# Three of twelve output projections by seven products of quarters instead of eight (Strassen, one level)

## The chip, the cores and the metric

The kernel runs on one core of a Trainium2 chip. The metric is device time in microseconds for one execution; 8 runs of the kernel before are given by their median. A core has a matrix engine (TensorE, PE in the profile), a vector engine (DVE), a scalar engine (ACT), GpSimd (POOL) and a queue engine that issues DMAs (SP). Each engine works through its own queue in order; semaphores hold an instruction until its inputs are there. Matmuls write to PSUM[...]; everything else here is in SBUF.

## What is computed

Four batches, eight heads, 768 tokens, head dimension 64. Queries and keys are each assigned to one of 16 clusters; attention is masked to pairs of the same cluster. The result, 3072 tokens by 512, goes through a two-layer network. All of it is f32.

```python
scores = np.where(mask, scale * np.matmul(q, k.transpose(0, 1, 3, 2)), -1e9)
attn = softmax(scores); x = (attn @ v) as (B*S, H*D)     # 3072 x 512
h = x @ w_in                                             # 512 -> 2048
sp = np.maximum(h, 0.0) + np.log1p(np.exp(-np.abs(h)))
g = h * erf(sp)
out = g @ w_out                                          # 2048 -> 512
```

The change is in the last line, `g @ w_out`.

## The kernel before

Heads are worked in 16 pairs (p), each in two halves of 384 queries and six key tiles of 128: a "unit" is one pair, half and key tile, 192 in all. Attention's outputs land transposed in tiles `xT`. The two-layer network works on chunks of 256 tokens, three to a batch, twelve in all (`NCHUNK = 12`, `CPB = 3`, `TB = 256`); chunks 9, 10 and 11 are the last batch's.

For a chunk n, `hidden(n)` (line 599) makes the hidden layer: eight groups of two 128-row feature tiles, each the sum of four matmuls 256 columns wide into a PSUM tile `hp`, which DVE copies into the tile `g` (16 feature tiles x 256 tokens; two buffers). After the last group `gate(n)` (line 567) puts Softplus and Erf on ACT, half a chunk at a time, and multiplies on POOL; chunk 11's products are on DVE. `project(n)` (line 623) then makes the output: for each of two token tiles, 16 matmuls 512 columns wide add up in one PSUM bank `po`, DVE copies it to `osb`, and SP stores it. `w_out` is a resident tile of 16 feature tiles by 512.

The order of the network's matmuls comes from one generator, `ffn_stream` (line 643). It runs hidden(n) and, after the first 16 matmuls, slips in two matmuls of project(n-1) behind each one of hidden(n). While attention runs, this stream is drawn in portions (`pump`) between units; after the last unit, a closing loop draws the rest: by the plan's count that is chunk 8's projection and the hidden layers and projections of chunks 9, 10 and 11. The first part of the program is pinned to the written order (`InOrder`, `in_order`); from there on a planner orders each engine's queue, with the written order as priority, and puts in all waits.

The tiles that the change borrows belong to attention: `prs` (eight tiles of exponentials, two planes of 384 each), `lows` (bf16 operands of query and key), `rowp` (transposed queries and keys, two buffers of each), `vp` (values, two buffers), `accp` (row sums, two buffers), `stage` (loaded queries and keys), and in PSUM `ps_s` (scores, two buffers of two banks). Operations made through `InOrder` all carry line 61 in the profile, so groups there are told apart by their tiles.

Of the kernel before, what the change touches and what calls it, by code (L numbers as in the profile page):

```python
# [9 lines left out]
F32 = mybir.dt.float32  # L10
# [4 lines left out]
ALU = mybir.AluOpType  # L15
# [4 lines left out]
P = 128  # L20
B, H, S, D = 4, 8, 768, 64
C = 16
NJ = S // P
Q = 32
NB = S // Q
HW = S // 2
HJ = NJ // 2
HP = H // 2
NPAIR = B * HP
DM, DFF = H * D, 2048  # L30
NFT = DFF // P
GW = 2
TB = 256
NCHUNK = B * S // TB
# [35 lines left out]
def kernel(  # L70
# [10 lines left out]
    nc = tc.nc  # L81

    in_order = [True]
    te, ve, ae, ge = (
        InOrder(tc, e, in_order) for e in (nc.tensor, nc.vector, nc.scalar, nc.gpsimd)
    )

    def pool(name, bufs, **kw):
        return ctx.enter_context(tc.tile_pool(name=name, bufs=bufs, **kw))

    const = pool("const", 1)
    stage = pool("stage", 1)
    vp = pool("vp", 2)
    rowp = pool("rowp", 2)
    routep = pool("routep", 1)
    small = pool("small", 2)
    accp = pool("accp", 2)
# [4 lines left out]
    ps_s = pool("ps_s", 2, space=PSUM)  # L102
# [10 lines left out]
    w_out = const.tile([P, NFT, DM], F32, name="w_out")  # L113
# [6 lines left out]
    lows = [  # L120
        {nm: const.tile([P, 2, S], BF16, name=f"{nm}m{i}") for nm in "qk"} for i in range(2)
    ]

    prs = [const.tile([P, 2, HW + 2], F32, name=f"pr{i}") for i in range(NPT)]
# [46 lines left out]
    for base, pattern, sign, op, fill in (  # L171
# [5 lines left out]
            out=first, in_=first, compare_op=op, fill=fill, base=base, pattern=pattern,  # L177
# [94 lines left out]
    for it in range(2):  # L272
# [4 lines left out]
            out=twice, in0=ss, scalar=inv, in1=norm, op0=ALU.mult, op1=ALU.add  # L277
# [3 lines left out]
            out=norm, in0=twice, scalar1=0.5, scalar2=(1e-6 if it else 0.0),  # L281
# [240 lines left out]
    def divide(u):  # L522

        p, half, _ = units[u]
        st = pairs[p]
        av = st["av", half]

        psum = ps_x.tile([P, HW], F32, name="psum", tag="x")
        for e in range(2):
            te.matmul(  # L530
                psum[e * D : (e + 1) * D], lhsT=minus, rhs=st["acc", half][:, e], start=True, stop=True
            )

        inv = routep.tile([P, HW], F32, name="inv")
        den = routep.tile([P, HW], F32, name="den")
        ae.activation(out=inv, in_=psum, func=ACT.Ln, bias=alleps, scale=-1.0)
        ae.activation(out=inv, in_=inv, func=ACT.Exp, scale=-1.0)
        yield
        ve.scalar_tensor_tensor(
            out=den, in0=psum, scalar=S * EPS, in1=inv, op0=ALU.subtract, op1=ALU.mult  # L540
        )
        ve.scalar_tensor_tensor(
            out=den, in0=den, scalar=2.0, in1=inv, op0=ALU.add, op1=ALU.mult
        )
        x = xTs.setdefault(p, {})
        lo = half * HW
        while lo < (half + 1) * HW:
            c = lo // TB
            hi = min((c + 1) * TB, (half + 1) * HW)
            if c not in x:  # L550
                x[c] = xTp.tile([P, TB], F32, name=f"xT{c}", bufs=XBUFS[c])
            mine = slice(lo - half * HW, hi - half * HW)
            ve.scalar_tensor_tensor(
                out=x[c][:, lo - c * TB : hi - c * TB], in0=av[:, mine], scalar=av[:, HW : HW + 1],
                in1=den[:, mine], op0=ALU.add, op1=ALU.mult,
            )
            lo = hi
        done.add((p, half))
        if half == 1:
            del pairs[p]  # L560
        yield


    TJ = TB // P
    CPB = S // TB
# [25 lines left out]
    def gate_products(n=NFT):  # L591
        for product in gating[:n]:
            product()
        del gating[:n]

    gs = {}
    resting = [0]

    def hidden(n):
        b, c = n // CPB, n % CPB  # L600
        gs[n] = gp.tile([P, NFT, TB], F32, name="g")
        for fp in range(NFT // GW):
            while converted[0] < DM // P * (fp * GW * P // LC + 1):
                yield None
            hp = ps_x.tile([P, GW, TB], F32, name="hp", tag="x")
            for a in range(GW):
                f0 = (fp * GW + a) * P
                for r in range(HP):
                    te.matmul(
                        hp[:, a], lhsT=w_in[:, r, f0 : f0 + P],  # L610
                        rhs=xTs[b * HP + r][c],
                        start=(r == 0), stop=(r == HP - 1),
                    )
                    if (a, r) != (GW - 1, HP - 1):
                        yield 4 * TB
            ve.tensor_copy(out=gs[n][:, fp * GW : (fp + 1) * GW], in_=hp)
            if fp == NFT // GW - 1:
                gate(n)
            yield 4 * TB

    out_v = out.rearrange("(b j p) m -> b j p m", p=P, j=NJ)

    def project(n):
        b, c = n // CPB, n % CPB
        gate_products()
        for tt in range(TJ):
            po = ps_x.tile([P, DM], F32, name="po", tag="x")
            for ft in range(NFT):
                while converted[0] < n_w_in + ft + 1:
                    yield None  # L630
                te.matmul(
                    po, lhsT=gs[n][:, ft, tt * P : (tt + 1) * P], rhs=w_out[:, ft],
                    start=(ft == 0), stop=(ft == NFT - 1),
                )
                if ft < NFT - 1:
                    yield 4 * DM
            osb = outp.tile([P, DM], F32, name="osb")
            ve.tensor_copy(out=osb, in_=po)
            nc.sync.dma_start(out=out_v[b, c * TJ + tt], in_=osb)
            yield 4 * DM  # L640
        del gs[n]

    def ffn_stream():


        late = iter(())
        for n in range(NCHUNK):
            b, c = n // CPB, n % CPB
            halves = range(c * TB // HW, ((c + 1) * TB - 1) // HW + 1)
            while not all((b * HP + r, h) in done for r in range(HP) for h in halves):  # L650
                yield None
            i = 0
            for cost in hidden(n):
                yield cost
                i += cost is not None
                if n > 1 and i > 2 * GW * HP:
                    for _ in range(2):
                        if (x := next(late, None)) is not None:
                            yield x
            yield from late  # L660
            late = project(n)
        yield from late

    stream = ffn_stream()
    pumped = [0]

# [35 lines left out]
    for e in range(2):  # L702
        ve.tensor_copy(
            out=ccT[e * D : (e + 1) * D, :, e * C : (e + 1) * C],
            in_=pct[e * D : (e + 1) * D].rearrange("d (r e c) -> d r e c", e=2, c=C)[:, :, e],
# [11 lines left out]
    for e in range(2):  # L717
        ve.reduce_sum(
            out=own[:, e : e + 1],
            in_=ident.rearrange("p (g x c) -> p x g c", x=2, c=C)[:, e], axis=AX.XY,  # L720
# [13 lines left out]
    for slot in range(2 * NJ * HP):  # L734
        in_order[0] = slot < FIRST
        p, r = divmod(slot, 2 * NJ)
# [40 lines left out]
    for u in range(2 * NJ * HP, len(units), 2):  # L777
        p, half, j = units[u]
# [24 lines left out]
        attend(n)  # L803
    for _ in divide(len(units) - 1):
        pass
    while next(stream, None) is not None:
        pass

# [31 lines left out]
```

## Time and profile before

| | |
|---|---|
| median of 8 runs | 1198.52 us (1193.54 to 1200.39) |
| profiled execution | 1199.88 us, of which the span is 1198.2 us |
| granted TensorE clock, mean over the span | 0.984 |
| matmuls of the hidden layer (`hp`) | 1536 records, 388.5 us busy |
| matmuls of the projections (`po`) | 768 records, 367.8 us busy |
| last attention matmul, in the trace | about 1001.5 us |
| projections of chunks 9, 10, 11 | 1064.0 to 1098.0, 1119.1 to 1153.1, 1166.9 to 1194.5 us; the first two interleaved with the next hidden layer |
| last store issued | 1195.28 us |

The span runs from the first to the last instruction; the rest of the execution's time lies around it. One f32 matmul of the code leaves two records. "Busy" is the union of the records of a group, "mean" the length of one record, and matmuls overlap in the pipeline: the spacing of starts, not the mean length, is what one costs in a row. In the forty slices a digit is the busy share in tenths.

### The profile page before, as it was taken

What the parts mean: (1) busy time and instruction counts of PE and PEld (TensorE: products, weight loads), DVE (VectorE), ACT (ScalarE), POOL (GpSimd) and SP (SyncE); (2) the same over time, 40 slices, a digit from 0 to 9 for tenths busy, and PEclk for the clock granted to TensorE, in tenths of its full rate; (3) what the DMA queues carried; (4) which work ended last, traced back from release to release, by engine and by line L of the source; (5) the groups of instructions that cost most, each with busy time, mean ns of one, the idle gap of its engine ahead of it and who ended that gap; (6) DMA issues with size and microseconds to landing.
All of it is one profiled execution on the core that took longest, in us unless ns stands there. A gap on an engine that the chain in (4) does not pass through costs nothing.

```text
span 1198.2 us, 13349 instructions
## 1 busy us (share of the span) xinstructions
PE 1151.5 (96%) x4912; PEld 619.8 (52%) x4912; DVE 515.8 (43%) x971; ACT 587.3 (49%) x682; POOL 461.6 (39%) x466
## 2 busy tenths in 40 slices
PE   4999978999999989999999999999999999999998
PEld 1233356654544554564474455565456456576663
DVE  7778885635443544343462434334354012111121
ACT  5889897863525363471553454164355253222222
POOL 3677764554333424161353243144244253031100
PEclk8999989899999899999999999999999999999999
DMA  7652443110202010020201101020000000000000
GB/s 137 164 128 40 99 152 58 53 27 23 43 15 27 23 27 22 9 40 1 45 14 17 35 14 33 9 36 14 10 23 1 9 9 1 18 1 18 8 10 18
DMA packets 140561, 42.95 MB, mean 36 GB/s; under 512 B 133328, under 2 KB 133328, under 8 KB 140496
## 3 DMA queue, kind: packets, MB, share of 16 engines
q1 hardware_dynamic: 137360, 41.70, 15.6%
q10 hardware_dynamic: 3136, 0.39, 0.3%
q8 instruction: 39, 0.64, 0.2%
q14 instruction: 26, 0.21, 0.1%
HBM read 35.68 MB, written 6.29 MB: 35 GB/s over the span
## 4 chain that ended last, share of the span: by engine, by line
PE 78%; ACT 8%; issue 7%; DVE 4%; DMA 2%; SPq 0%; POOL 0%; ACTq 0%; DVEq 0%; POOLq 0%
PE hp L61 25%; PE po L61 25%; PE sc L61 13%; PE av L61 8%; PE sm L61 4%; ACT w_out L61 2%; ACT L61 2%; DVE nmx L61 1%; ACT km L61 1%; PE psim L61 1%; PE psum L61 1%; DMA in_q<-in_q_dram 1%; ACT pr L61 1%; ACT inv L61 1%; ACT a_s L61 1%
## 5 line engine op out<-in xcount | busy, mean ns | idle before, releaser
L61 PE MATMUL hp<-xT,w_in 128*128 128x256 f32 x1536 | 388.5, 390 | 7.9 <-DVE xT L61 6.2
L61 PE MATMUL po<-w_out,g 128*128 128x512 f32 x768 | 367.8, 597 | 0.6 <-DVE den L61 0.6
L61 PEld LDWEIGHTS hp<-xT,w_in 128*128 128x128 f32 x1536 | 290.1, 194 | 130.0 <-issue 84.4
L61 POOL TENSOR_TENSOR acc<-acc,pr 128x384 f32<-128x384 f32 x256 | 236.3, 954 | 290.5 <-ACT pr L61 290.3
L61 DVE TENSOR_REDUCE nmx<-sm 128x1 f32<-128x384 f32 x384 | 195.8, 550 | 148.0 <-PE sm L61 147.1
L61 ACT ACT_TABLE_LOAD x110 | 141.1, 1283 | 231.9 <-DVE g L61 128.8
L61 ACT ACTIVATE pr<-sc 128x768 f32<-128x768 f32 x192 | 147.0, 806 | 147.1 <-PE sc L61 146.9
L61 PEld LDWEIGHTS po<-w_out,g 128*128 128x128 f32 x768 | 141.8, 190 | 106.9 <-issue 94.1
L61 POOL TENSOR_TENSOR g<-a_s,g 128x512 f32<-128x512 f32 x88 | 111.4, 1298 | 216.5 <-ACT a_s L61 216.5
L61 PE MATMUL sc<-qT,kT 64*128 64x384 f32 x768 | 181.8, 528 | 4.8 <-ACT pr L61 4.7
L61 DVE COPY g<-hp 128x512 f32<-128x512 f32 x96 | 65.9, 687 | 255.1 <-PE hp L61 254.7
L61 PE MATMUL av<-pr,in_v 128*64 128x386 f32 x768 | 139.9, 496 | 0.0
L61 PE MATMUL sm<-km,qm 128*128 128x384 bf16 x384 | 103.2, 336 | 14.4 <-DVE nmx L61 4.1
L61 PEld LDWEIGHTS sc<-qT,kT 64*128 64x128 f32 x768 | 69.9, 188 | 82.3 <-issue 47.0
L61 POOL TENSOR_TENSOR acc<-pr,pr 128x384 f32<-128x384 f32 x64 | 65.4, 1043 | 92.8 <-ACT pr L61 92.8
L61 PEld LDWEIGHTS av<-pr,in_v 128*64 128x64 f32 x768 | 49.2, 136 | 80.1 <-issue 70.1
L61 PEld LDWEIGHTS <-qm 128*128 128x128 bf16 x384 | 34.8, 99 | 81.8 <-issue 66.8
L61 DVE SCALAR_TENSOR_TENSOR den<-psum,inv 128x384 f32<-128x384 f32 x32 | 17.8, 557 | 129.2 <-ACT inv L61 128.8
L61 ACT ACTIVATE w_out<-w_out 128x512 int32<-128x512 uint32 (+2 forms) x68 | 62.0, 952 | 2.1 <-DMA w_out<-in_moe_w_out_dram 1.7
L61 ACT ACTIVATE a_s<-g 128x2048 f32<-128x2048 f32 x24 | 45.8, 1910 | 32.5 <-DVE g L61 32.3
L61 PE MATMUL sc<-qm,km 64*128 64x384 bf16 x384 | 60.1, 328 | 0.0
L61 ACT COPY nmT<-pn 6x128 bf16<-6x128 bf16 x31 | 7.7, 248 | 95.1 <-PE pn L61 95.1
(75 smaller groups left out, 605.5 us busy)
## 6 DMA issues: line engine op xcount, KB each, us to landing
w_out<-in_moe_w_in_dram SPq DMA_DIRECT2D x16, 512.0 KB, 6.6
in_q<-in_q_dram SPq DMA_DIRECT2D x64, 96.0 KB, 3.1
in_v<-in_v_dram SPq DMA_DIRECT2D x32, 192.0 KB, 3.0
w_out<-in_moe_w_out_dram SPq DMA_DIRECT2D x12, 512.0 KB, 3.6
out_dram<-osb SPq DMA_DIRECT2D x24, 256.0 KB, 2.0
in_k<-in_k_dram SPq DMA_DIRECT2D x60, 96.0 KB, 3.4
qm<-nmT SPq DMA_DIRECT2D x186, 0.2 KB, 1.7
a_s<-in_moe_w_out_dram SPq DMA_DIRECT2D x4, 512.0 KB, 3.4
```

The costliest lines, as they stand in the source:

```text
L61: ins = getattr(self.engine, name)(*args, **kw)
```

## The change

For chunks 9, 10 and 11 `project` is replaced by `project_fast`. It cuts `g` in quarters (token tile x feature half) and `w_out` in quarters (feature half x output half), and makes the four output quarters from seven products of sums and differences of quarters. Each product is eight matmuls 256 wide.

- `add_weights`, written after the last unit and ahead of the closing loop, makes three sums of weight quarters (24 adds of 128x256, every fourth on POOL) in planes of `prs` and `lows`.
- `subtract_weights`, written after chunk 8's projection, replaces two weight quarters in place by differences.
- `add_hidden(n)`, at the head of each `project_fast(n)`, makes three sums of hidden quarters (in tiles of `rowp`, or of `vp` and `accp`) and replaces two quarters of `g` in place by differences, all on DVE.
- The products are collected in the two `ps_s` buffers and put together by DVE in two tiles of `stage`; an output quarter is stored as soon as it is done, so a chunk has four stores of 128x256 instead of two of 128x512.
- The hidden layers of chunks 10 and 11 have no projection slipped in; each projection runs in one piece behind the next hidden layer.

```diff
+    FAST = NCHUNK - CPB
+    HF, HM = NFT // 2, DM // 2
+    def g_part(n, tt, fh):
+        return gs[n][:, fh * HF : (fh + 1) * HF, tt * P : (tt + 1) * P]
+    def w_part(fh, mh):
+        return w_out[:, fh * HF : (fh + 1) * HF, mh * HM : (mh + 1) * HM]
...
+    def add_weights():
+        planes = [t[:, e, 0:HM] for t in prs for e in range(2)]
+        planes += [
+            t[nm].bitcast(F32)[:, e, 0:HM] for t in lows for nm in "qk" for e in range(2)
+        ]
+        for name, (x, y) in {"++": ((0, 0), (1, 1)), "0+": ((0, 0), (0, 1)), "1+": ((1, 0), (1, 1))}.items():
+            w_sum[name] = [planes.pop(0) for _ in range(HF)]
+            for f in range(HF):
+                (ge if f % 4 == 3 else ve).tensor_tensor(
+                    out=w_sum[name][f], in0=w_part(*x)[:, f], in1=w_part(*y)[:, f], op=ALU.add
+                )
+    def subtract_weights():
+        for x, y in (((0, 1), (1, 1)), ((1, 0), (0, 0))):
+            for f in range(0, HF, 2):
+                ve.tensor_tensor(
+                    out=w_part(*x)[:, f : f + 2], in0=w_part(*x)[:, f : f + 2],
+                    in1=w_part(*y)[:, f : f + 2], op=ALU.subtract,
+                )
+    def add_hidden(n):
+        if n % 2:
+            tiles = [rowp.tile([P, S], F32, name=nm + "T") for nm in "qkqk"]
...
+        lot = S // P
+        sums = g_sum[n] = {}
+        for i, (name, x, y) in enumerate(
+            (("+1", (1, 0), (1, 1)), ("0+", (0, 0), (0, 1)), ("++", (0, 0), (1, 1)))
+        ):
...
+            for fs, o in ((slice(0, lot), tiles[i]), (slice(lot, HF), tiles[3][:, rest])):
+                ve.tensor_tensor(out=o, in0=g_part(n, *x)[:, fs], in1=g_part(n, *y)[:, fs], op=ALU.add)
+        for x, y in (((1, 0), (0, 0)), ((0, 1), (1, 1))):
+            ve.tensor_tensor(out=g_part(n, *x), in0=g_part(n, *x), in1=g_part(n, *y), op=ALU.subtract)
+    def project_fast(n):
...
+        add_hidden(n)
...
+        def product(o, g, w):
+            for f in range(HF):
+                te.matmul(
+                    o, lhsT=g[f] if isinstance(g, list) else g[:, f],
+                    rhs=w[f] if isinstance(w, list) else w[:, f], start=(f == 0), stop=(f == HF - 1),
+                )
+                yield 4 * HM
...
+        yield from product(m3, g_part(n, 0, 0), w_part(0, 1))
+        yield from product(m4, g_part(n, 1, 1), w_part(1, 0))
+        yield from product(m2, gsum["+1"], w_part(0, 0))
+        yield from product(m5, gsum["0+"], w_part(1, 1))
+        ve.tensor_copy(out=so_far(0, 1), in_=m3)
+        ve.tensor_copy(out=so_far(0, 0), in_=m4)
+        put(1, 0, so_far(0, 0), m2, ALU.add)
+        put(1, 1, so_far(0, 1), m2, ALU.subtract)
+        put(0, 1, so_far(0, 1), m5, ALU.add)
+        put(0, 0, so_far(0, 0), m5, ALU.subtract)
...
+        yield from product(m6, g_part(n, 1, 0), w_sum["0+"])
+        yield from product(m7, g_part(n, 0, 1), w_sum["1+"])
+        put(1, 1, so_far(1, 1), m6, ALU.add)
+        put(0, 0, so_far(0, 0), m7, ALU.add)
+        yield from product(m1, gsum["++"], w_sum["++"])
+        for tt in range(TJ):
+            put(tt, tt, so_far(tt, tt), m1, ALU.add)
+            nc.sync.dma_start(
+                out=out_v[b, c * TJ + tt, :, tt * HM : (tt + 1) * HM], in_=so_far(tt, tt)
+            )
+        del gs[n]
...
-                if n > 1 and i > 2 * GW * HP:
+                if 1 < n <= FAST and i > 2 * GW * HP:
...
-            late = project(n)
+            if n == FAST:
+                subtract_weights()
+            late = (project if n < FAST else project_fast)(n)
...
+    add_weights()
     while next(stream, None) is not None:
```

More of the change, by code (lines that the diff above doesn't have):

```diff
@@ L641, in project @@
         del gs[n]
+    FAST = NCHUNK - CPB
[4 more added lines that the diff above has]
+        return w_out[:, fh * HF : (fh + 1) * HF, mh * HM : (mh + 1) * HM]
+    w_sum = {}
+    g_sum = {}
+    def add_weights():
[9 more added lines that the diff above has]
+                )
@@ new lines, in subtract_weights @@
+    def subtract_weights():
[8 more added lines that the diff above has]
+            tiles = [rowp.tile([P, S], F32, name=nm + "T") for nm in "qkqk"]
+        else:
+            tiles = [vp.tile([P, NJ, 2, D], F32, name="in_v") for _ in range(2)]
+            tiles = [t.rearrange("p j e d -> p (j e d)") for t in tiles]
+            tiles += [
+                accp.tile([P, 2, HW], F32, name="acc").rearrange("p e n -> p (e n)") for _ in range(2)
+            ]
+        tiles = [t.rearrange("p (f t) -> p f t", t=P) for t in tiles]
+        lot = S // P
[3 more added lines that the diff above has]
+        ):
+            rest = slice(i * (HF - lot), (i + 1) * (HF - lot))
+            sums[name] = [tiles[i][:, f] for f in range(lot)] + [tiles[3][:, f] for f in range(rest.start, rest.stop)]
+            for fs, o in ((slice(0, lot), tiles[i]), (slice(lot, HF), tiles[3][:, rest])):
+                ve.tensor_tensor(out=o, in0=g_part(n, *x)[:, fs], in1=g_part(n, *y)[:, fs], op=ALU.add)
+        for x, y in (((1, 0), (0, 0)), ((0, 1), (1, 1))):
+            ve.tensor_tensor(out=g_part(n, *x), in0=g_part(n, *x), in1=g_part(n, *y), op=ALU.subtract)
@@ new lines, in project_fast, with put, so_far @@
+    def project_fast(n):
+        b, c = n // CPB, n % CPB
+        add_hidden(n)
+        gsum = g_sum[n]
+        one = ps_s.tile([P, 2, 512], F32, name="sc", tag="s").rearrange("p e (h m) -> p (e h) m", h=2)
+        two = ps_s.tile([P, 2, 512], F32, name="sc", tag="s").rearrange("p e (h m) -> p (e h) m", h=2)
+        osb = [
+            stage.tile([P, NB, Q], F32, name="in_" + nm).rearrange("p n t -> p (n t)")[:, 0:DM] for nm in "qk"
+        ]
+        def product(o, g, w):
[5 more added lines that the diff above has]
+                yield 4 * HM
+        def put(tt, mh, x, y, op):
+            ve.tensor_tensor(out=osb[tt][:, mh * HM : (mh + 1) * HM], in0=x, in1=y, op=op)
+        def so_far(tt, mh):
+            return osb[tt][:, mh * HM : (mh + 1) * HM]
+        m3, m4, m2, m5 = (one[:, i] for i in range(4))
+        m6, m7, m1 = (two[:, i] for i in (0, 1, 2))
+        yield from product(m3, g_part(n, 0, 0), w_part(0, 1))
[10 more added lines that the diff above has]
+            nc.sync.dma_start(
+                out=out_v[b, c * TJ + tt, :, (1 - tt) * HM : (2 - tt) * HM], in_=so_far(tt, 1 - tt)
+            )
[4 more added lines that the diff above has]
+        yield from product(m1, gsum["++"], w_sum["++"])
+        for tt in range(TJ):
+            put(tt, tt, so_far(tt, tt), m1, ALU.add)
+            nc.sync.dma_start(
+                out=out_v[b, c * TJ + tt, :, tt * HM : (tt + 1) * HM], in_=so_far(tt, tt)
+            )
+        del gs[n]
```

## The prediction

> **What bounds the kernel now.** I read the share of busy time first, then the forty slices, then the stretch that the change touches, then the chain of waits at the end.
>
> ```profile
> PE 1151.5 (96%) x4912; PEld 619.8 (52%) x4912; DVE 515.8 (43%) x971; ACT 587.3 (49%) x682; POOL 461.6 (39%) x466
> PE   4999978999999989999999999999999999999998
> DVE  7778885635443544343462434334354012111121
> PEclk8999989899999899999999999999999999999999
> ```
>
> TensorE is the bound on average, and the slices say more: from slice 33 of 40 on PE is full, its clock is full, and VectorE (DVE) is at a tenth or two. That last stretch is where the change lies. By stretches there (columns: length; busy time and instructions of PE, weight loads, DVE, ACT, POOL; granted clock; DMA share; GB/s):
>
> ```profile
> 1057.00:1084.00 27.00, 27.00 (x90) 16.83 (x89) 3.36 (x5) 6.39 (x4) 4.94 (x4) 1.00 0.03 10
> 1084.00:1111.00 27.00, 27.00 (x100) 18.69 (x99) 3.46 (x5) 6.39 (x4) 4.94 (x4) 1.00 0.03 10
> 1139.00:1167.00 28.00, 28.00 (x105) 19.58 (x104) 5.86 (x9) 6.39 (x4) 0.00 (x0) 1.00 0.03 10
> ```
>
> PE never stops, and every other engine is idle for four fifths of the time. The chain that ended last closes it (start, length, what):
>
> ```profile
> 1153.24 13.81 PE hp L61 x64
> 1167.05 27.48 PE po L61 x64
> 1194.53 0.02 issue
> 1194.56 0.69 DVE osb L61
> ```
>
> Nothing but matmuls, one behind the other, then one copy and the last store. So a matmul taken out of this stretch comes off the end time in full, as long as nothing new makes PE wait.
>
> **The sum on TensorE.** The trace has two records for each f32 matmul of the code. One projection is 2 token tiles x 16 matmuls 512 wide = 32 matmuls = the 64 records of 27.48 us: 0.8588 us each. A matmul 256 wide is known from the hidden layer: 64 records, 32 matmuls, 13.81 us: 0.4316 us each, with a new weight tile at every one, as the new products have. Check: from 1043.05 us (end of chunk 8's projection, in the chain) to 1194.53 there lie 160 hidden matmuls and 96 of projection: 160 x 0.4316 + 96 x 0.8588 = 151.5 us, and the stretch is 151.48. The two prices explain all of it.
>
> After the change a projection is 7 products x 8 matmuls = 56, 256 wide: 56 x 0.4316 = 24.17 us. Saved per projection 27.48 - 24.17 = 3.31 us; three of them: **9.93 us**. One eighth of the work is 12.5%; of 27.48 us I get 12.0%, because two 256-wide matmuls (0.8632) cost 4 ns more than one 512-wide.
>
> A rule of the Trainium skill speaks against cutting matmuls in half: "TensorE: Matmul & The Clock Gate", section "Back-to-back issue gap", has a fixed cost of about 2.5 ns in each pass beside N/2.4, and "FP8 and Floating Point Precision", section "TensorE Precision Notes", counts 4 passes for true f32. By the rule, as an estimate, 512 wide is 4 x 215.8 = 863 ns and 256 wide 4 x 109.2 = 437 ns: 32 x 0.863 - 56 x 0.437 = 3.15 us saved, 9.5 in all. The rows give 9.9. The floor is there in the trace, but smaller (4 ns, not 10), and I take the rows.
>
> Start of a product: 21 products begin behind waits on sums, where a hidden group of four matmuls begins behind a PSUM buffer. The 98 records at 1042.89 took 21.15 us in the chain, 0.4316 each across some twelve such starts, so a start costs nothing that can be seen. Upper bound: the 0.17 us by which a closed run of 64 records outlasts its share of the chain (13.98 against 13.81), x 21 = 3.6 us. I take 0, the nearer row.
>
> **The sums, and what hides them.** No add of two SBUF f32 tiles of these widths runs in the trace. The nearest row is the gate's product, 128x512, 686 ns alone and 0.63 us in a row (4 in 2.50); from it I estimate 0.63 x width/512 + 0.05: 256 wide 0.37, 768 wide 1.0, 1024 wide 1.3 us. (From the other side 0.48, the 128x256 operation that reads PSUM.)
> - add_weights: 18 adds on DVE, 18 x 0.37 = 6.6 us, and 6 on POOL at some 0.7 (954 ns for 384 wide), 4 us. They come after the last attention products, about 1001 us. From 1010 to 1024 us DVE and POOL do nothing before; the sums are wanted some 80 us later. POOL's last four gate products of chunk 8 (1003.2 to 1008.2) can slip by 2 to 3 us; the projection that reads them starts at 1008.95 with other quarters. Cost 0.
> - subtract_weights: 8 of 512 wide, 5 us on DVE, once chunk 8's projection has read w_out (1043). First needed at 1084. Cost 0.
> - add_hidden, each chunk: 3 x (1.0 + 0.37) + 2 x 1.3 = 6.7 us of DVE. Now the timetable. The hidden layers of chunks 10 and 11 are no longer interleaved with projections, so PE runs chunk 9's rest to 1056.9, hidden 10 to 1084.5, projection 9 to 1108.7, hidden 11 to 1136.3, projection 10 to 1160.5, projection 11 to 1184.6. A gate is done 12 us after its last hidden matmul where POOL multiplies (1057 to 1069.1), about 10 where DVE does (0.7 + 6.4 of ACT + 2.5). So the sums of 9 are ready at 1069 + 6.7 = 1076 (wanted at 1084.5), of 10 at 1103 (1136.3), of 11 at 1146 + 6.7 = 1153 (1160.5). Slack 8, 33 and 8 us. Cost 0; and products m3 and m4, which need no sum of the hidden layer, cover another 16 x 0.4316 = 6.9 us.
>
> A second rule is against this: "GPSIMD Engine Reference", section "Specifications", says that POOL shares its SBUF interfaces with DVE instructions that have two SBUF inputs, and all these adds have two. The gate of chunk 9 has eight POOL products, 9.9 us by the row; if DVE's 5 us of weight subtraction stopped POOL outright, chunk 9's sums would come at 1081 rather than 1076: still before 1084.5. Rule and row give the same end time.
>
> - Stores: six more of 256 columns, each some 0.36 us on SP's queue, which in this stretch holds nothing else. Cost 0.
> - Hidden buffers: there are two, so hidden 11 needs chunk 9's buffer, free after m7; m1 and the first hidden group (8 matmuls each, 6.9 us together) lie between that and its first write. Cost 0.
> - PSUM: the products use the two score buffers, free since attention ended; each is read by DVE at least 8 us before the next projection writes it.
> - The end: before, one copy of 0.69 us and one store (issued in 0.33 us). After, two DVE adds of a 256-wide PSUM half (0.48 each by the row of that width) and two stores of half the size; the second leaves 0.27 us later. Bounds -0.1 and +0.6; I take **+0.3 us**.
>
> Sum: 9.93 - 0.3 = 9.6 us off the span of 1198.2, so 1188.6; the profiled execution took 1199.88, which makes 1190.3. The median of the runs is 1.36 us below that execution: **1189.0 us**.
>
> **Rivals.** All turn on the order in DVE's queue. As the code is written, the sums of chunk n come behind all copies and gate products of hidden layer n+1. The order executed is not the written one:
>
> ```profile
> 1156.73 0.69 DVE L61 COPY g<-hp 128x512 f32<-128x512 f32 x1 [2.76 <-PE hp L61]
> 1158.79 1.90 DVE L61 TENSOR_TENSOR g<-a_s,g 128x512 f32<-128x512 f32 x3 [1.37 <-ACT a_s L61]
> 1160.60 0.68 DVE L61 COPY g<-hp 128x512 f32<-128x512 f32 x1
> 1161.20 0.68 DVE L61 TENSOR_TENSOR g<-a_s,g 128x512 f32<-128x512 f32 x1
> 1163.63 0.69 DVE L61 COPY g<-hp 128x512 f32<-128x512 f32 x1 [1.75 <-PE hp L61]
> ```
>
> Chunk 11's gate products are written behind its last copy, yet four run before the last two. The planner pulls work forward into idle time, so I expect the same for the sums.
>
> 1. Forecast, sums pulled forward, no wait: 1189.0. Chance 0.80.
> 2. Written order, but waits by region. Chunks 9 and 11 lose nothing (first sum ready 2 us in, wanted 6.9 in). Chunk 10's sums stand behind chunk 11's gate products: first sum at 9.8 + 1.4 = 11.2 us, wanted at 6.9: 4.3 us lost. 1193. Chance 0.06. Starts that cost 0.17 us each give 1192.6, chance 0.05.
> 3. Slower: written order, and m3 has to wait for the in-place subtraction because the two interleaved halves of the hidden tile count as one range. Then each projection stands still for its whole set of sums: chunk 9 for 0.7 + 6.7 = 7.4, chunk 10 for 9.8 + 6.7 = 16.5, chunk 11 for 7.2: 31 us lost for 9.6 won, 1220. It decides from 9.6 us of waiting on. For it: in-place writes in strided halves are new here. Against it: the order above, and that project(11) began on the first half of g (1166.89) while DVE wrote the second (1174.3), so waits are not by whole tiles. With this and partial forms of it: 0.06.
> 4. It does not do what it says: the seven products run, but earlier work is ordered anew and gives the gain back. The new instructions come last in the program, so they only fill idle time; 0.03, about 1198.
>
> **Numbers.** A measurement tells 0.3%, 3.6 us, from no change. Cases 1 and 2 are faster: 0.91, less a little for waits that add up: 0.90; same 0.04; slower 0.06. The range runs from 1185 (the runs of before spread from 1193.5 to 1200.4, so another median of them can lie some 4 us lower) to 1194 (case 2).
>
> **What will show it.** 168 matmuls, 336 records, of 256 columns in place of 192 records of 512; PE at full share from 1057 to about 1185; in DVE's order each chunk's five sums ahead of the next hidden layer's last copies; the last matmul near 1184.6 and 3.9 us from there to the end. A gap on PE ahead of m3 or m2 would show rival 3 or 2; PE without gaps but a price above 0.4316 us would mean the width costs more here than in the hidden layer.

## The result, and the profile after

| | before | after |
|---|---|---|
| median | 1199.02 us (32 runs, 1193.46 to 1206.86) | 1186.86 us (11 runs, 1184.21 to 1191.84) |
| ratio to before, 95% interval | | 0.9914 (0.9895 to 0.9932) |
| profiled execution: time, span | 1199.88, 1198.2 us | 1191.08, 1189.4 us |
| stretch: first hidden matmul behind the last attention product to the end of the last matmul | 193.03 us | 184.26 us |
| from there to the end of the span | 3.67 us | 3.72 us |

Faster by 0.86%; the forecast was 1189.0 us, from 1185 to 1194. Single runs of one kernel lie up to 13 us apart (the last section has one cause), so the experiments are read by the stretch in the table. Each stretch comes from one profiled execution, but it repeats well: in before, after and runs 1 and 3 it is within 0.3 us of its matmuls at the prediction's two prices plus the wait named below, and runs 6 and 7, which have the same waits, agree to 0.01 us. Ahead of it the change adds only the sums of weights on DVE and POOL. They cost TensorE nothing: from 760 us to the stretch, each of its instructions lies at the same distance from its place in before, to 0.01 us. First the page of the changed kernel, its shares and slices:

```profile
PE 1141.4 (96%) x5056; PEld 646.5 (54%) x5056; DVE 556.7 (47%) x1045; ACT 587.3 (49%) x682; POOL 467.2 (39%) x472
PE   5999978899999989999999999999999999999998
DVE  7788885636443534334263345334445215134351
PEclk9999989999999989999999999999999999999999
```

TensorE has 144 records more (336 for 192) and 10 us less of work; its share of the shorter span is still 96%. DVE has gone from a tenth or two to as much as five in the last slices: those are the sums, and PE's row does not show them. The chain that ended last shows what is new (start, length, what; the products carry the name sc of the score buffers, m1 to m7 are the seven products in the diff, and DVE's sums of products go to in_q and in_k):

```profile
1136.21 44.91 PE sc L61 x208
1181.12 0.02 issue
1181.14 0.42 DVE in_k L61
1181.56 0.34 DVE in_q L61
1181.91 0.04 issue
1181.95 3.73 PE sc L61 x16
1185.68 0.02 issue
1185.71 0.42 DVE in_q L61
```

The 104 matmuls of 44.91 us cost 0.4318 us each, the price of the hidden layer. But the chain leaves PE once: between the end of m7 at 1181.12 and the start of m1 at 1181.95 lie two DVE adds, and m1's eight matmuls take 3.73 us where eight at 0.4316 are 3.45. That is 1.1 us of the 9.9 that the matmuls saved. Last, DVE's order in time, for chunk 9 (copies of the hidden layer of chunk 10 between the sums of chunk 9):

```profile
1070.97 0.68 DVE L61 COPY g<-hp 128x512 f32<-128x512 f32 x1
1071.57 0.41 DVE L61 TENSOR_TENSOR kT<-g 128x256 f32<-128x256 f32 x1
1071.91 0.94 DVE L61 TENSOR_TENSOR qT<-g 128x768 f32<-128x768 f32 x1
...
1074.85 1.21 DVE L61 TENSOR_TENSOR g<-g 128x1024 f32<-128x1024 f32 x1
1075.98 0.68 DVE L61 COPY g<-hp 128x512 f32<-128x512 f32 x1
```

The sums are written behind all eight copies and stand among them: pulled forward, done at 1076.06, and the projection that wants them starts at 1084.25.

### The profile page after: what moved, and what is told of

Its sections match the earlier page's. It is cut to its first block, busy times and chain, and to the rows that moved or that the text cites. A ratio compares the mean times of both kernels' runs of the same rounds, so it can differ in the third digit from the quotient of the medians.

```text
span 1189.4 us, 13756 instructions
## 1 busy us (share of the span) xinstructions
PE 1141.4 (96%) x5056; PEld 646.5 (54%) x5056; DVE 556.7 (47%) x1045; ACT 587.3 (49%) x682; POOL 467.2 (39%) x472
## 4 chain that ended last, share of the span: by engine, by line
PE 76%; ACT 9%; issue 7%; DVE 5%; DMA 2%; POOL 1%; SPq 0%; DVEq 0%; ACTq 0%; POOLq 0%
PE hp L61 25%; PE sc L61 19%; PE po L61 18%; PE av L61 7%; PE sm L61 4%; ACT w_out L61 2%; ACT km L61 2%; ACT L61 2%; DVE nmx L61 2%; PE psim L61 1%; ACT pr L61 1%; PE psum L61 1%; DMA in_q<-in_q_dram 1%; ACT inv L61 1%; DVE den L61 1%
## 5 line engine op out<-in xcount | busy, mean ns | idle before, releaser
L61 PE MATMUL hp<-xT,w_in 128*128 128x256 f32 x1536 | 382.4, 389 | 8.1 <-DVE xT L61 6.4
L61 PE MATMUL po<-w_out,g 128*128 128x512 f32 x576 | 280.1, 598 | 0.6 <-DVE den L61 0.6
L61 PEld LDWEIGHTS po<-w_out,g 128*128 128x128 f32 x576 | 105.3, 190 | 75.1 <-issue 64.2
L61 ACT ACTIVATE a_s<-a_s 128x2048 f32<-128x2048 f32 (+2 forms) x32 | 53.9, 1685 | 0.4
```

The lines of the kernel that those rows point to most:

```text
L61: ins = getattr(self.engine, name)(*args, **kw)
```

## The experiments

In each, the stretch of the table above is compared; the ratios are to before. Between before and after it fell by 8.77 us; the matmuls alone account for 9.93.

**1. m1 in a PSUM buffer of its own.** Of the four quarters of the second score buffer (two banks of 512 columns), m6 and m7 lie in one bank and m1 in the other. The new buffer comes from the ring of four (`ps_x`) that also holds the hidden layer's `hp`.

```diff
-        m6, m7, m1 = (two[:, i] for i in (0, 1, 2))
+        m6, m7 = (two[:, i] for i in (0, 1))
+        m1 = ps_x.tile([P, HM], F32, name="m1", tag="x")
```

> Product m1 gets a PSUM buffer of its own instead of a quarter of the buffer that also holds m6 and m7; nothing else differs. Theory A (the 0.84 us gap of TensorE ahead of chunk 11's m1, and the slow restart behind it, are a wait for DVE to have read m6 and m7 out of the same buffer): the gap goes, the 64 records of chunk 11's last products run at 0.4316 us a matmul without a break, the last matmul ends about 1.1 us earlier against the end of chunk 8's projection (141.6 us after it instead of 142.7). Theory B (m1 waits for something else, for its inputs or for the bank): the gap stays or moves, and the last matmul ends 142.7 us after it. The time itself moves by 0.1%, less than can be told from the runs.

The end of its chain:

```profile
1162.85 20.72 PE sc L61 x96
1183.57 3.47 PE m L61 x16
1187.04 0.02 issue
```

No DVE piece is left between m7 and m1, and m1 takes 3.47 us. The last matmul ends 141.60 us after chunk 8's projection; the stretch is 183.15 us, 9.88 below before. So theory A holds: m1, as the planner placed its waits, waited for DVE to have read m6 and m7 out of the same buffer, although it writes another bank of it. Time 1187.76 (5 runs), ratio 0.9907 (0.9873 to 0.9940), not to be told from the changed kernel.

**2. The written order in DVE's queue**, from the sums of weights on.

```diff
+    ve.on = [True]
     add_weights()
```

> The changed kernel, with DVE's queue held to the order of the code from the sums of weights on; the other engines are ordered as before. If the forecast's theory holds (the sums cost nothing because the planner pulls them ahead, and waits go by regions, not by whole tiles): chunks 9 and 11 lose nothing, since m3 and m4 cover the first sums; at chunk 10 the sums stand behind chunk 11's gate products, the first is ready some 11.2 us after the hidden layer's end and wanted at 6.9, so TensorE stands still for about 4.3 us, and the time is 1191 to 1192. If waits take the strided halves of the hidden tile for one range (rival 3): 7.4 + 16.5 + 7.2 = 31 us of gaps, ahead of m3 each time, and 1218. If the planner's order does not matter (all hidden anyway): no gap, 1187.

TensorE at chunk 10 (start, length, what, idle time before), and the same moments by stretch (the columns as in the prediction; the clock is the number ahead of the last two):

```profile
1142.48 4.43 PE L61 MATMUL sc<-w_out,in_v 128*128 128x256 f32 x12 [3.78 <-DVE in_v L61]
```

```profile
1138.50:1142.40 3.90, 0.20 (x1) 0.00 (x0) 3.34 (x6) 0.53 (x1) 0.00 (x0) 0.99 0.00 0
1142.40:1144.00 1.60, 1.52 (x4) 1.25 (x5) 1.60 (x5) 0.00 (x0) 0.00 (x0) 0.50 0.00 0
1144.00:1147.00 3.00, 3.00 (x12) 2.49 (x11) 3.00 (x4) 0.00 (x0) 0.00 (x0) 0.71 0.03 5
```

One new gap behind chunk 8, where rival 2 had put it: ahead of m2 of chunk 10, 3.78 us for a forecast 4.3. There is none ahead of m3 anywhere, none at chunk 9, and at chunk 11 only the 0.84 us ahead of m1 that the changed kernel has too. But the gap cost more than its length: the granted clock is 0.50 behind it, and m2's first twelve records start to start take 4.27 us where chunk 10 of the changed kernel has 2.60. The Trainium skill, "TensorE: Matmul & The Clock Gate", section "HAM oscillation — how this bites in real kernels", says that idle gaps above about 3.4 us do this; here is one, of 3.78. The stretch is 190.48 us, 6.2 above the changed kernel's: 3.8 of gap, 1.7 of half clock, 0.6 already lost before chunk 8's projection ends (42.14 us from the stretch's start, against 41.55), half of it in a wait of 0.33 us behind DVE at its first matmul. So the planner's order carries some seven tenths of the gain. Time 1197.06 (20 runs), ratio 0.998 (0.9962 to 0.9997), where 1191 to 1192 was forecast; the profiled execution, 1192.32, is the fastest of the twenty, and what the others lost beyond its 6.2 us stays open.

**3. Eight products in the new order.** `project_fast` as a plain sum, each matmul cut in two, with no sums of quarters:

```diff
+            for mh in range(2):
+                for ft in range(NFT):
+                    te.matmul(
+                        po[:, mh * HM : (mh + 1) * HM], lhsT=gs[n][:, ft, tt * P : (tt + 1) * P],
+                        rhs=w_out[:, ft, mh * HM : (mh + 1) * HM], start=(ft == 0), stop=(ft == NFT - 1),
+                    )
```

> Chunks 9, 10 and 11 again by all eight products: the plain sum over 16 feature tiles, but each matmul cut to 256 columns (64 matmuls a projection) and the projections in one piece behind the next hidden layer, as in the changed kernel; no sums of quarters. If the gain is the eighth product left out, and width and order cost what the rows say: 3 x (64 x 0.4316 - 27.48) = 0.4 us slower than before in the stretch from chunk 8's projection to the last matmul (151.9 us), so no change in the time that can be told, ratio 1.000. If the new order by itself brought part of the gain: faster than before by up to that part. If the narrower matmul is dearer by the rule of 2.5 ns a pass: 1.3 us slower than before (152.8 us).

Stretch 193.51 us, 0.48 above before, forecast 0.4; the rule's 10 ns for each of the 96 matmuls cut in two would make 1.0. Time 1200.13 (12 runs), ratio 1.0002 (0.9985 to 1.0019). The width and the new order bring nothing and cost half a microsecond; the gain is the eighth product.

**4. The sums four times over.**

```diff
-            for fs, o in ((slice(0, lot), tiles[i]), (slice(lot, HF), tiles[3][:, rest])):
+            for fs, o in ((slice(0, lot), tiles[i]), (slice(lot, HF), tiles[3][:, rest])) * 4:
```

> Each of the hidden layer's three sums is made four times over instead of once, with the same result, so DVE has about 12 us more to do for each chunk ahead of the two in-place subtractions. If sums lie in slack and waits go by regions: chunk 9's subtractions end some 4 us after its m3 could start, chunk 11's as well, but m3 and m4 need none of them and m2's sum is there in time; no gap on TensorE ahead of m3, same time as the changed kernel within what can be told, 1187. If m3 waits for the in-place subtraction (one range): gaps of some 4 us ahead of m3 at chunks 9 and 11, 8 us in all, 1195. If DVE's time counts in full: 36 us, 1223.

No theory had this right (they said 1187, 1195 and 1223). DVE's order shows chunk 9's in-place subtractions and, later, the adds that read its m6 and m7:

```profile
1090.14 2.35 DVE L61 TENSOR_TENSOR g<-g 128x1024 f32<-128x1024 f32 x2
...
1115.77 1.28 DVE L61 TENSOR_TENSOR acc<-g 128x256 f32<-128x256 f32 x2
1116.98 0.41 DVE L61 TENSOR_TENSOR in_k<-in_k,sc 128x256 f32<-128x256 f32 x1
1117.31 0.41 DVE L61 TENSOR_TENSOR in_q<-in_q,sc 128x256 f32<-128x256 f32 x1
```

TensorE's shows its m3 and m4 and, later, its m1:

```profile
1084.25 7.07 PE L61 MATMUL sc<-w_out,g 128*128 128x256 f32 x32
...
1117.77 5.21 PE L61 MATMUL sc<-pr,qT 128*128 128x256 f32 x12 [10.91 <-DVE in_q L61]
```

m3 and m4 ran from 1084.25 to 1091.3. The in-place subtractions of the halves beside theirs in the same tile are written ahead of them, yet began only at 1090.1 and ended at 1092.5: waits on the hidden tile go by regions, and rival 3's premise is false. The loss is elsewhere. Chunk 10's sums, pulled forward as early as chunk 10's gate allowed (1103.4), stand in DVE's queue ahead of the adds that read m6 and m7 of chunk 9, and m1 waits for those: 10.9 us, and 2.5 us more at half clock (0.50 granted; its twelve records took 5.21 us for 2.75). Stretch 197.81, time 1204.15 (20 runs), ratio 1.004 (1.0024 to 1.0056).

**5. Both: sums four times over, m1 in its own buffer.**

> The sums four times over, as in the run before, and m1 in a PSUM buffer of its own. There the loss was a gap of 10.9 us ahead of chunk 9's m1, where DVE had still to read m6 and m7 out of the buffer that m1 shares, with chunk 10's repeated sums ahead of those two reads in its queue, and then matmuls at half clock. Theory A (DVE's added 36 us cost nothing by themselves; the loss is that shared buffer): the gap goes, TensorE runs without a break, last matmul 141.6 to 142.7 us after the end of chunk 8's projection, 1187. Theory B (DVE's work itself is too much for the slack): the gap moves to the next product that needs a sum or a buffer, and some 10 us or more remain, 1197 and up.

Stretch 185.30 us: of the 13.55 us lost in run 4, 11.4 are gone. One gap of 1.89 us is left, of a hidden matmul behind the DVE add that reads m1 (tile m). First that add, then TensorE:

```profile
1115.09 0.41 DVE L61 TENSOR_TENSOR in_k<-in_k,m 128x256 f32<-128x256 f32 x1
```

```profile
1103.14 10.52 PE L61 MATMUL hp<-xT,w_in 128*128 128x256 f32 x48
1115.55 14.73 PE L61 MATMUL hp<-xT,w_in 128*128 128x256 f32 x67 [1.89 <-DVE in_k L61]
```

Three hidden groups (48 records) fill the other three buffers of the ring, and the fourth needs m1's: again a PSUM buffer whose reader stands behind the sums. DVE is busy 34.5 us longer than in run 1 (590.8 against 556.3), and the stretch grows by 2.15. So theory A, nearly whole: DVE's added work costs almost nothing by itself; what waits behind it in its queue costs. Time 1190.9 (8 runs; 1187 was forecast), ratio 0.9931 (0.9907 to 0.9956).

**6 and 7. Chunk 8 as well; then m7 last.** Both keep m1's own buffer; in run 7 m7 has one too.

```diff
-    FAST = NCHUNK - CPB
+    FAST = NCHUNK - CPB - 1
...
+        gate_products()
...
+                while not weights_added[0]:
+                    yield None
                 subtract_weights()
```

> Chunk 8's projection by seven products as well, so four projections instead of three, and m1 in its own buffer. If a projection by seven products saves 3.31 us wherever TensorE is full and the sums find room: 3.3 us less than with m1's own buffer alone, 4.4 less than the changed kernel, 1182 to 1183, ratio to before 0.986 to 0.988. If chunk 8's sums, which now fall among the last divisions of attention, hold up DVE's queue there: gaps on TensorE around the end of attention, and the saving is smaller or gone.

In run 7 also:

```diff
+        yield from product(m1, gsum["++"], w_sum["++"])
+        for tt in range(TJ):
+            put(tt, tt, so_far(tt, tt), m1, ALU.add)
+        for tt, o, g, w in (
+            (1, m6, g_part(n, 1, 0), w_sum["0+"]), (0, m7, g_part(n, 0, 1), w_sum["1+"]),
+        ):
+            yield from product(o, g, w)
+            put(tt, tt, so_far(tt, tt), o, ALU.add)
...
```

> As the four-chunk version, with the products in the order m3, m4, m2, m5, m1, m6, m7, so that behind the last matmul only one output quarter is left to add and to store, in place of two. Expected: one DVE add (0.34 us) and one store's issue (0.4 us) less behind the last matmul, the end 0.4 to 0.8 us after it sooner than in the changed kernel (3.0 to 3.3 us instead of 3.7). Too little to be told in the runs' times: 1182, ratio to before 0.985 to 0.988. If the order makes a product wait for a buffer: a gap, up to 1 us for each chunk.

Both have a stretch of 180.95 us, 2.20 below run 1 where 3.31 was forecast, and both have a gap around 1009: a hidden matmul waits 0.82 us (0.83 in run 7) for a copy that DVE makes late. Ahead of that copy stand four weight subtractions; in run 7 (TensorE, DVE, POOL):

```profile
1009.97 2.21 PE L61 MATMUL hp<-xT,w_in 128*128 128x256 f32 x9 [0.83 <-DVE g L61]
```

```profile
1003.61 5.70 DVE L61 TENSOR_TENSOR w_out<-w_out 128x512 f32<-128x512 f32 x4
```

```profile
1003.69 6.75 POOL L61 TENSOR_TENSOR g<-a_s,g 128x512 f32<-128x512 f32 x4 [1.29 <-ACT a_s L61]
```

Four such adds take 2.5 us when POOL is quiet, and POOL's four 4.93. Run 7 ends 3.08 us behind its last matmul, not 3.72: one add and one store less, as forecast. Times: run 6 1187.67 (4 runs), ratio 0.990 (0.9869 to 0.9930); run 7 1183.47 (6 runs), ratio 0.9874 (0.9847 to 0.9900).

**8. Chunk 8's gate products on DVE instead of POOL.**

```diff
-                    (ge if n < NCHUNK - 1 else ve).tensor_tensor, out=h[:, i : i + GW],
+                    (ge if n not in (FAST, NCHUNK - 1) else ve).tensor_tensor, out=h[:, i : i + GW],
```

> As the four-chunk version with m7 last, but chunk 8's eight gate products are on DVE instead of POOL. In the four-chunk versions TensorE stands still for 0.8 us around 1009, waiting for a copy of hp that DVE makes late: ahead of it four weight subtractions of 128x512 took 5.70 us, which take 2.44 us when POOL is quiet, while four of POOL's gate products ran beside them (6.75 us instead of 4.93). Theory A (two-input operations of DVE and POOL hold each other up): with no gate product on POOL there, the four subtractions take 2.4 to 2.8 us, and the copy comes in time or nearly so: gap under 0.3 us, last matmul about 1 us earlier against the first hidden matmul behind the last attention product (179.9 us after it instead of 180.95). Theory B (DVE is late because it has too much to do there): 2.5 us of products more on DVE, the gap stays or grows. The time moves by 0.1% either way, which the runs cannot tell.

```profile
1003.94 2.48 DVE L61 TENSOR_TENSOR w_out<-w_out 128x512 f32<-128x512 f32 x4
```

With more to do, DVE is on time: the four subtractions take 2.48 us, the gap is gone, the stretch is 179.86 us, 3.29 below run 1, a whole projection's saving. Theory A; over the whole span DVE is busy 568.0 us with eight products more, against 567.8 in run 7. A little is lost ahead of the stretch in runs 6 to 8: a weight subtraction there delays another copy, and a hidden matmul around 993 us waits 1.11 us for DVE where it waits 0.78 in before, so each saves 0.33 us less than its stretch says. Time 1184.18 (4 runs), ratio 0.988 (0.9844 to 0.9915). Runs 7 and 8 are the fastest versions found; their stretches are 3.3 and 4.4 us shorter than the changed kernel's, a difference that the times of so few runs do not resolve.

## Why the prediction was right, and where it was off

- **The sum on TensorE** (9.93 us, from rows of two widths) held to 0.05 us: run 1, without the wait, saves 9.88. Run 3 shows that leaving out the eighth product is all of it. The fixed cost of a narrower matmul is the 4 ns of the rows, not the rule's 10 (the section gives its cost for an isolated matmul, and these stand in a row).
- **"PSUM: the products use the two score buffers ... each is read by DVE at least 8 us before the next projection writes it"** is the step that failed. It looked from one projection to the next and not inside one: m1 writes the buffer that m6 and m7 have just left, behind two DVE adds. Cost 1.1 us at chunk 11. At chunks 9 and 10 three matmuls of other work stand between m7 and m1 and cover it. Between projections the room was there, though smaller than said: the first buffer of chunk 10 was read by 1154.0, and chunk 11's m3 wrote it from 1156.8.
- **The end**, +0.3 us, was 0.05: the step of two adds and two smaller stores was priced too high.
- **The sums and their timetable** held: chunk 9's ready at 1076.06 (forecast 1076), chunk 10's at 1102.5 (1103), chunk 11's at 1152.5 (1153). That the first fits to 0.1 us is luck: chunk 9's sums began 1.2 us before the gate's forecast end and took 8.2 us instead of 6.7, with two copies among them and the first sum slowed beside POOL. The weights' sums came not at 1001 us but from 924 to 1003, between attention's operations. ACT, counted among the engines idle for four fifths of the time, was busy for 6.39 us of 27, which changes nothing. Run 5 shows how thick the cover is, run 4 how it can be lost.
- **The rivals**: the order in DVE's queue was the right thing to turn on. Rival 2's gap came where and nearly as long as said once the written order was forced (3.78 for 4.3), but its price left out the clock. Rival 3 has no ground: run 4 shows waits by region on the hidden tile (the PSUM buffer of m1 is another case).
- **The rule on POOL and DVE** was weighed only for a POOL that is stopped. Both slow down; nothing in the changed kernel's chain lies behind it, so the end time was right, but runs 6 to 8 show a place where it costs 1.1 us.
- **The sum against the profile**: forecast 9.6 us of span, measured 8.8: 9.93, less 1.1 for the wait, and 0.05 less at the end. The medians lie 12.2 apart and the ratio of the runs says 10.3 (8.2 to 12.6); 8.8 lies inside that interval, so the runs show no gain that the stretch leaves unexplained. That the median came out 2.1 us below the forecast, although the change saved a little less than forecast, is the spread of the runs, and luck.

## What to carry to other kernels

Where one engine is full and the rest idle, count its instructions and price them by the trace's own rows of the same width; that sum was good to a per cent here, and the work that pays for it elsewhere is free as long as nothing urgent stands behind it in its queue. So look not for how much a helper engine has to do, but for who waits for the instruction at the end of its queue: a PSUM buffer shared by products that are read and written in turn made 35 us of harmless sums cost 13.6. And when a wait is priced, add the clock: a gap of 3.8 us cost 5.5.

## What the runs showed of the hardware

**DVE and POOL hold each other up** when both work on two SBUF inputs: an add of 128x512 took 1.42 us instead of 0.62 beside a POOL product, and the product 1.69 instead of 1.23 (run 7). They nearly take turns: alone, four adds and four products are 2.48 and 4.94 us, 7.4 one after the other; together they took 6.8. In the changed kernel it was DVE that stood back: its first sum of chunk 9 took 2.00 us instead of 0.95 beside POOL's last gate product, while POOL's four took 4.94.

**A gap of 2.7 us sometimes halves the clock and sometimes not.** Before and run 3 are the same program up to the network's last chunks. Around 425 us TensorE waits 2.67 us for ACT in both. In before, then in run 3:

```profile
429.29 2.93 PE L61 MATMUL hp<-xT,w_in 128*128 128x256 f32 x6
```

```profile
426.67 1.56 PE L61 MATMUL hp<-xT,w_in 128*128 128x256 f32 x6
```

The same six records, at half speed and at full. A little earlier (396 to 406 us) the granted clock is 0.66 in before and 1.00 in run 3. At 396 us run 3 is 0.6 us behind before, at 435 us 4.2 us ahead, and 5.8 us when the stretch begins. So this wait costs its length, or 1.6 us more (before) or 3.0 us more (the changed kernel), and the times of one kernel spread.

The ten traces show when. In each, the changes of clock lie on a grid of 3.41 us, which lies elsewhere in every execution. In before a step of that grid ends at 429.19 (the columns as in run 2):

```profile
425.78:429.19 3.41, 0.77 (x4) 0.30 (x4) 0.69 (x1) 3.38 (x5) 0.68 (x1) 1.00 0.00 0
429.19:432.60 3.41, 3.41 (x10) 2.30 (x10) 0.00 (x0) 0.29 (x1) 2.91 (x4) 0.50 0.00 0
```

The wait of 2.67 us is in all ten, and half clock follows in seven, from the end of the step on. In those seven 1.82 us or more of the wait fall into one step; in the other three (runs 2, 3 and 5) at most 1.72. At a wait around 190 us, 2.8 to 3.3 us long, the limit lies elsewhere: up to 2.05 us in one step no half clock, from 2.10 on there is. So it is a matter of where the gap falls, but these figures are no general threshold. The Trainium skill, "TensorE: Matmul & The Clock Gate", section "Part 1: The HAM clock gate", has a window that runs freely and is not tied to the kernel's start; the grid in these traces agrees with it. But half clock after 2.67 us of waiting goes beyond the 3.4 us that run 2 names from that page, and the measurement decides. No run moved a gap on purpose to test it.
